# An attention and soft-mixture kernel: the value products' bank stored in two halves by two engines, and the inverse row sums kept in PSUM

## The chip, the cores and the metric

The kernel runs on one core of a Trainium2 chip. The metric is the device time of one execution in microseconds; lower is better. The engines are named as in the profile: PE is TensorE (matrix products and transposes, results in PSUM), DVE is VectorE, ACT is ScalarE, POOL is GpSimd, SP is SyncE, which here only issues DMAs. Each engine works through its own instructions in the order in which the program lists them. PSUM has banks of 512 float32 columns on 128 partitions.

## The reference

Eight batches of eight heads of windowed attention (576 positions, head size 64, window 128, a linear bias with the distance), then a soft mixture of experts over all 4608 tokens:

```python
scores = scale * np.matmul(q, k.transpose(0, 1, 3, 2))
scores = np.where(mask, scores + bias[None], -1000000000.0)   # mask: 0 <= i - j < 128
attn = np.exp(scores - np.max(scores, axis=-1, keepdims=True))
attn = attn / (np.sum(attn, axis=-1, keepdims=True) + 1e-09)
x = np.matmul(attn, v)                                        # -> tokens x 512
logits = x @ phi                                              # 32 slots, 4 for each expert
d = softmax over tokens;  slot_input = d.T @ x
slot_out[e] = np.maximum(slot_input[e] @ w1[e], 0.0) @ w2[e]
c = softmax over slots;   out = c @ slot_out
```

## The kernel before, in words

**Groups and turns.** A tile is 128 positions of one batch; each batch has four (t = 0 to 3) and a short tail tile of 64 (t = 4). The work goes by groups `(b, t, g)`: a full tile has two groups (g = 0 and 1) of four heads each, the tail tile has one with all eight. That makes nine groups a batch and 72 in all. The main loop makes one turn for each group `i`, and a turn works on several groups at once, at different stages. The order in which the loop's lines stand is the order on each engine; nothing is reordered.

**One turn**, after the first seven, lists:

1. `softmax_front` for the new group i and the old one i-1. On DVE: `merge` (L286, selects the valid score blocks, in PSUM), `rowmax` (L300, into a corner of the score bank), `inverse` of the old row sums (L313), `bias` (L304, the negated maximum times the scale), `normalise` of the old group (L317, the exponentials times the inverse sums, in SBUF). `total` (L309, row sum plus epsilon) runs on POOL.
2. `flip` of group i-3: PE transposes its probabilities into columns 0 to 255 of the two banks of `pq` (L374). Columns 256 to 511 of these banks take the transposed outputs of finished tiles (`x_flip`, L438).
3. `split` of group i-3: ACT copies the flipped probabilities to SBUF (L380), POOL masks them into two operands (L386, L388).
4. ACT work put down for this turn under "act": `x_keep` (L447, copies a flipped output tile to SBUF) and copies of the token steps (`token_copy` L464, `token_keep` L507).
5. `values` of group i-4: 16 products on PE (L410) into the bank `xp`. Then `after_values`.
6. `scores` of group i+1 on PE (L261 the bias terms, L270 the products) into one of two score buffers of two banks each, `s4_0` and `s4_1`, used in turn.
7. `expo` of group i: four ACT exponentials out of the score banks (L359), each with its row sum. It needs `bias` of this turn.
8. PE work put down under "pe": `x_flip` of a tile one turn or more after its last group's products, and, for every fourth tile, the token steps: `logits` (L456), `slot_flip` (L477) and `token_flip` (L502), both into a bank called `dp`, `slot_sum` (L514). On DVE, `slots_max` reads `dp` (L536, L537) and `slot_add` is L522.

**Values and their copy.** Both groups of a tile write the same bank `xp`, four pairs of heads side by side. When the second group (or the tail tile) is done, `x_store` copies the bank to SBUF on DVE (L424), in program order after the turn's normalisation. The next tile's first group takes a new `xp`, which is the same bank again.

**After the loop** the last groups are finished in an order written out by hand, in free score banks and in `pq`, and then come the experts' products with weights streamed in by DMA.

The row sums `rs` are a small SBUF tile; their inverse is written in place and read by `normalise` as an operand that is repeated over 128 columns.

## Time and profile before

| | before |
|---|---|
| time, median of 3 runs | 286.24 us (286.18 to 286.52) |
| the profiled execution's time | 286.09 us |
| its span, first to last instruction | 284.3 us |
| busy PE / DVE / ACT / POOL | 257.5 / 218.6 / 190.5 / 111.7 us |
| mean granted TensorE clock | 0.992 |
| bytes read / written in HBM | 62.30 / 9.44 MB |

The loop takes about the first 215 us of the span, the experts the rest. In rows of a timeline the columns are start, duration, engine, line, operation, output and inputs, count, and in brackets the idle time ahead of the instruction with what ended it. PEld is PE's loading of stationary operands, which runs beside its products. In rows of groups they are the shape and count, then busy time and mean ns of one, then the idle time ahead. In rows of waits: total us, times, longest. In rows of one window: start and end, length, busy time and count of PE, PEld, DVE, ACT and POOL (or of the one engine asked for), granted clock, share of DMA time, GB/s.

### The profile page before, as it was taken

To read this page: it belongs to the slowest core of one execution; us is meant where nothing else is said; L and a number is where in the kernel's file an instruction comes from. 1 tells how busy PE (TensorE), PEld (TensorE's weight loads), DVE (VectorE), ACT (ScalarE), POOL (GpSimd) and SP (SyncE) were. 2 spreads that over 40 slices of the span, in tenths; PEclk is the share of its full clock that TensorE was granted. 3 is DMA by queue.
4 is the path that set the end of the run, shared out by engine and by line. 5 is a ranking of instruction groups with operands and counts; after the bars stand their busy time and mean duration, and the time that the engine had idled before them with its cause. 6 is when DMAs were issued, how large, how long until landed. Compare 5 with 4: busy or idle time off the path is not lost.

```text
span 284.3 us, 11675 instructions
## 1 busy us (share of the span) xinstructions
PE 257.5 (91%) x4575; PEld 180.7 (64%) x4575; DVE 218.6 (77%) x546; ACT 190.5 (67%) x780; POOL 111.7 (39%) x221
## 2 busy tenths in 40 slices
PE   7789898989899999998989998998989899999990
PEld 3567676767577677676667766766666443587750
DVE  1789998997998898899999899897973352656352
ACT  2868868887798887897897888887774411044460
POOL 3035734481574385265527526556452011000000
PEclk9999999999999999999999999999999999999996
DMA  5735368889786998889698778876565588999997
GB/s 167 238 110 153 115 173 250 255 247 295 252 277 184 303 303 262 257 265 285 221 298 283 255 236 280 268 212 218 166 213 199 172 257 296 417 416 373 376 357 295
DMA packets 36767, 72.49 MB, mean 255 GB/s; under 512 B 4413, under 2 KB 15337, under 8 KB 36713
## 3 DMA queue, kind: packets, MB, share of 16 engines
q1 hardware_dynamic: 35992, 71.25, 75.7%
q8 instruction: 36, 0.59, 0.8%
q10 hardware_dynamic: 720, 0.51, 0.6%
q14 instruction: 19, 0.15, 0.2%
HBM read 62.30 MB, written 9.44 MB: 252 GB/s over the span
## 4 chain that ended last, share of the span: by engine, by line
PE 44%; DVE 38%; ACT 9%; issue 3%; DMA 3%; POOL 1%; DVEq 0%; ACTq 0%; SPq 0%; POOLq 0%
DVE area L317 12%; DVE s L300 9%; PE xp L410 8%; ACT area L359 6%; PE op L967 5%; PE s L270 5%; DVE area L424 5%; PE hp L930 5%; DVE s L286 4%; PE po L992 4%; PE s L261 2%; PE lp L456 2%; PE pq L374 2%; DVE acc L522 2%; DMA area<-v_n 2%
## 5 line engine op out<-in xcount | busy, mean ns | idle before, releaser
L359 ACT ACTIVATE area<-s,nb 128x128 f32<-128x128 f32 x286 | 101.9, 379 | 21.6 <-DVE nb L304 20.2
L410 PE MATMUL xp<-area 128*64 128x128 f32 (+1 forms) x1104 | 71.7, 270 | 9.5 <-DVE area L424 6.6
L410 PEld LDWEIGHTS xp<-area 128*64 128x64 f32 x1104 | 54.5, 137 | 16.4 <-POOL area L388 5.0
L359 ACT ACTIVATION_READ_ACCUMULATOR area<-s,nb 128x1 f32 x286 | 62.2, 218 | 0.0
L317 DVE TENSOR_TENSOR area<-area,rs 128x512 f32<-128x512 f32 (+1 forms) x73 | 59.9, 821 | 1.7 <-ACT area L447 0.4
L270 PE MATMUL s<-kq 64*64 64x192 f32 (+2 forms) x1144 | 57.0, 316 | 0.0
L386 POOL TENSOR_SCALAR_AFFINE_SELECT area<-area 128x512 f32<-128x512 f32 (+1 forms) x57 | 42.7, 748 | 26.9 <-ACT area L380 26.3
L380 ACT COPY area<-pq 128x512 f32<-128x512 f32 (+1 forms) x72 | 42.5, 592 | 16.0 <-PE pq L374 14.3
L300 DVE TENSOR_REDUCE s<-s 128x4 f32<-128x512 f32 (+1 forms) x72 | 50.0, 694 | 2.2
L388 POOL TENSOR_SCALAR_AFFINE_SELECT area<-area 128x512 f32<-128x512 f32 (+1 forms) x57 | 46.5, 817 | 3.9
L270 PEld LDWEIGHTS s<-kq 64*64 64x64 f32 x1144 | 41.2, 139 | 3.4
L309 POOL TENSOR_SCALAR rs<-sm 128x4 f32<-128x4 f32 x70 | 13.5, 193 | 71.2 <-ACT area L359 69.8
L286 DVE COPY_PREDICATED s<-cst,s 128x256 f32<-128x256 int32 (+1 forms) x72 | 30.2, 419 | 4.8 <-PE s L270 4.4
L374 PE MATMUL pq<-unit_r,area 64*128 64x64 f32 x552 | 31.4, 234 | 1.9 <-ACT area L322 1.2
L374 PEld LDWEIGHTS pq<-unit_r,area 64*128 64x128 f32 x552 | 23.0, 140 | 11.6 <-issue 5.0
L261 PE MATMUL s<-ramp,pair_of 64*64 64x384 bf16 x286 | 27.0, 358 | 2.5 <-ACT area L359 2.0
L424 DVE COPY area<-xp 128x512 f32<-128x512 f32 (+1 forms) x38 | 24.1, 633 | 3.6 <-PE xp L410 3.4
L447 ACT COPY area<-pq 128x512 f32<-128x512 f32 x34 | 20.2, 594 | 0.3 <-PE pq L432 0.3
L261 PEld LDWEIGHTS <-pair_of 64*64 64x64 bf16 x288 | 9.5, 106 | 15.7 <-issue 12.0
L438 PEld LDWEIGHTS pq<-unit_r,area 64*128 64x128 f32 x264 | 10.7, 138 | 13.2 <-issue 11.7
L994 ACT COPY ob<-po 128x512 f32<-128x512 f32 x19 | 10.4, 592 | 11.4 <-PE po L992 11.4
L994 DVE COPY ob<-po 128x512 f32<-128x512 f32 x17 | 11.2, 686 | 6.6 <-PE po L992 4.4
(164 smaller groups left out, 276.6 us busy)
## 6 DMA issues: line engine op xcount, KB each, us to landing
w<-w SPq DMA_DIRECT2D x53, 512.0 KB, 5.4
out<-ob SPq DMA_DIRECT2D x36, 256.0 KB, 3.6
kq<-q_t SPq DMA_DIRECT2D x69, 128.0 KB, 3.3
kq<-k_t SPq DMA_DIRECT2D x32, 256.0 KB, 3.4
area<-v_n SPq DMA_DIRECT2D x31, 256.0 KB, 4.5
area<-w SPq DMA_DIRECT2D x8, 512.0 KB, 4.9
area<-v_n SPq DMA_DIRECT2D x12, 128.0 KB, 5.2
kq<-w SPq DMA_DIRECT2D x3, 512.0 KB, 5.6
```

The lines of the kernel that those rows point to most:

```text
L261: nc.tensor.matmul(dst[strip], lhsT=pair_of[rows, int(t == 0), strip], rhs=src, start=True, stop=False)
L270: nc.tensor.matmul(parts[par][KB * jj:KB * jj + KB, second * u + KB * skip:second * u + WIN], lhsT=qt[rows, jj if t < 4 else j, KB * h:KB ...
L286: nc.vector.copy_predicated(to, keep, of)
L300: nc.vector.tensor_reduce(st[key]["mx"], merged(key, us), axis=AX.X, op=ALU.max, negate=True)
L317: nc.vector.tensor_tensor(p4, p4, bc(rs, 2, P), op=ALU.mult)
L359: nc.scalar.activation(s["p4"][:, u], src, AF.Exp, bias=s["nb"][:, u:u + 1], scale=SCALE, accum_out=s["sm"][:, u:u + 1],)
L374: nc.tensor.transpose(s["pt"][:, 2 * (u % 2) + u // 2, r], s["p4"][rows, u], ident[rows, rows])
L380: nc.scalar.copy(pa[:, us].rearrange("p u (r w) -> p u r w", r=2), s["pt"][:, us])
L386: nc.gpsimd.affine_select(prev, own, [[-step, m], [0, 4], [-1, KB]], ALU.is_gt, 0.0, base=-i0, channel_multiplier=1)
L388: nc.gpsimd.affine_select(own, own, [[step, m], [0, 4], [1, KB]], ALU.is_ge, 0.0, base=i0, channel_multiplier=-1)
L410: nc.tensor.matmul(xp[D * par:D * par + D, j, 0:w], lhsT=v_slot[b, t - 1 + ph][:, D * h:D * h + D], rhs=src[:, :, par, i] if t < 4 else sr ...
L424: nc.vector.tensor_copy(dst, src[:, :, 0:w])
```

## The change

1. One tile `xp` is kept for the whole loop as two halves of 256 columns. Group number n writes half n mod 2, with a fresh start of its own sum, and each group's half is copied by itself. The copy of a first group (g = 0 of a full tile) is put down for the next turn under "act" and runs on ScalarE, after whatever was put down there before. The copy of a second group or of a tail tile stays on VectorE, in its own turn, with half the columns.
2. From the third turn on the inverse row sums of the old group are written to columns 504 to 507 of the new group's first score bank, and `normalise` reads them there.
3. After the loop each copy names its group; that of tile 3's second group has half the columns.

```diff
-    def inverse(key, us):
-        nc.vector.reciprocal(st[key]["rs"][:, us], st[key]["rs"][:, us])
+    def inverse(key, us, beside=None):
+        sums = st[key]["rs"]
+        if beside is not None:
+            st[key]["rs"] = st[beside]["s4"][:, 0, 4 * P - 8:4 * P - 4]
+        nc.vector.reciprocal(st[key]["rs"][:, us], sums[:, us])
...
-            inverse(old, ALL)
+            inverse(old, ALL, new)
...
     def values(key, pairs=None, to=None):
-        if (b, t) not in st or to is not None:
-            st[b, t] = ps_1.tile([P, NPAIR, P], F32, tag="xp", name="xp") if to is None else to
-        xp = st[b, t]
+        if ("x", key) in st:
+            xp = st["x", key]
+        elif to is None:
+            if not xp_bank:
+                xp_bank.append(ps_1.tile([P, 2, 2 * P], F32, tag="xp", name="xp"))
+            xp = xp_bank[0][:, number[key] % 2].rearrange("p (j w) -> p j w", j=2 if t < 4 else 4)
+        else:
+            xp = to[:, 2 * g:2 * g + 2] if t < 4 else to
+        st["x", key] = xp
...
-                        xp[D * par:D * par + D, j, 0:w], lhsT=v_slot[b, t - 1 + ph][:, D * h:D * h + D],
+                        xp[D * par:D * par + D, i, 0:w], lhsT=v_slot[b, t - 1 + ph][:, D * h:D * h + D],
...
-                        start=(fresh and (ph, i) == (parts[0], inner[0])), stop=(done and (ph, i) == (parts[-1], inner[-1])),
+                        start=((ph, i) == (parts[0], inner[0])), stop=((ph, i) == (parts[-1], inner[-1])),
...
-    def x_store(b, t, eng=None, js=slice(0, NPAIR)):
-        src = st[b, t][:, js]
+    def x_store(key, eng=None):
+        b, t, g = key
+        src = st.pop(("x", key))
...
-        dst = x_of(b, t)[:, js, o:o + w]
+        dst = x_of(b, t)[:, 2 * g:2 * g + src.shape[1], o:o + w]
...
     def after_values(i, key):
         b, t, g = key
+        if g == 0 and t < 4 and i + 1 < n:
+            do("act", i + 1, x_store, key, nc.scalar)
+        else:
+            x_store(key)
         if not (g == 1 or t == 4):
             return
...
-        x_store(b, t)
...
-        x_store(last, 3)
+        x_store(ga)
...
-        x_store(last, 4, nc.scalar)
+        x_store(gb, nc.scalar)
...
-        x_store(last, 0, nc.scalar, slice(0, 2))
+        x_store(gc, nc.scalar)
...
-        x_store(last, 0, js=slice(2, 4))
+        x_store(gd)
```

## The prediction

> **What bounds the kernel now.** The page first, for the span and the shares; then one window over the attention loop, whole and for the row maximum alone, which runs once for each group of heads and so counts the turns.

> ```profile
> span 284.3 us, 11675 instructions
> PE 257.5 (91%) x4575; PEld 180.7 (64%) x4575; DVE 218.6 (77%) x546; ACT 190.5 (67%) x780; POOL 111.7 (39%) x221
> PE 44%; DVE 38%; ACT 9%; issue 3%; DMA 3%; POOL 1%; DVEq 0%; ACTq 0%; SPq 0%; POOLq 0%
> L410 PE MATMUL xp<-area 128*64 128x128 f32 (+1 forms) x1104 | 71.7, 270 | 9.5 <-DVE area L424 6.6
> 30.00:210.00 180.00, 169.53 (x3331) 123.79 (x3331) 164.44 (x404) 146.85 (x639) 95.64 (x180) 1.00 0.77 243
> 30.00:210.00 180.00, 43.96 (x63) 1.00 0.77 243
> ```

> From 30 to 210 us TensorE is busy for 169.53 of 180 us (the first busy column), so PE is idle for 10.5 us in the whole stretch. 63 turns in 180 us make 2.86 us a turn, 5.7 us for the two turns of one tile. The chain divides itself between PE and DVE, but there is little slack in PE: what the change can give back in the loop is at most those idle microseconds, and a new wait of PE is paid nearly in full. Of the idle time, 9.5 us over the whole run lie ahead of the value products (L410), 6.6 of it because the bank's copy on VectorE (L424) is not done. That wait is what the halves speak to.

> **Does the program let two engines work in one bank at different columns?** All of the change hangs on this. Three places in the timeline show it, where the columns differ and no data is shared.

> ```profile
> 92.55 0.33 PE L502 MATMUL dp<-unit_r,lg 128*128 128x128 f32 x1
> 92.91 0.29 DVE L536 TENSOR_REDUCE cm<-dp 128x4 f32<-128x128 f32 x1 [0.39 <-PE dp L502]
> ...
> 138.06 0.66 ACT L380 COPY area<-pq 128x512 f32<-128x512 f32 x1
> 138.30 0.29 DVE L537 TENSOR_TENSOR ln<-dp,cm 128x128 f32<-128x128 f32 x1
> 138.62 0.27 ACT L507 COPY dn<-dp 128x128 f32<-128x128 f32 x1
> ...
> 97.22 0.58 ACT L447 COPY area<-pq 128x512 f32<-128x512 f32 x1
> 97.88 0.33 PEld L374 LDWEIGHTS pq<-unit_r,area 64*128 64x128 f32 x8 [0.28 <-ACT area L447]
> ...
> PEld pq L374 <- ACT area L447: 2.3, 9, 0.3
> ```

> L536 reads columns 256 up of dp, which another product wrote a turn before; L502 writes columns 0 to 127. L536 starts 0.03 us after L502 ends (92.88). So a read waits for a write elsewhere in its bank. L507 reads columns 0 to 127 of the same bank while L537 reads 256 up: it starts 0.03 us after L537 ends (138.59), so two reads wait for each other too. L374 writes pq's columns 0 to 255 while L447 reads 256 to 511, and waits for it 9 times. That is the situation of the two halves of xp, one engine on each. [...]

> **The change part by part.**

> *The first group's copy, on ScalarE.* It is put behind the split (L380) and the keep (L447) of the next turn, and ahead of that turn's value products in the program. Those write the other half of the bank, so they now wait for ScalarE. Before, the second group added into the same bank and waited for no copy. The stretch of a second group:

> ```profile
> 112.51 0.46 PE L374 MATMUL pq<-unit_r,area 64*128 64x64 f32 x8
> 112.89 1.10 PE L410 MATMUL xp<-area 128*64 128x128 f32 x16
> 113.08 0.59 ACT L380 COPY area<-pq 128x512 f32<-128x512 f32 x1 [1.22 <-PE pq L374]
> 113.57 0.59 ACT L447 COPY area<-pq 128x512 f32<-128x512 f32 x1
> ...
> L380 ACT COPY area<-pq 128x256 f32<-128x256 f32 x3 | 1.0, 368 | 0.7 <-PE pq L369 0.7
> ...
> 108.32 0.68 DVE L424 COPY area<-xp 128x512 f32<-128x512 f32 x1
> 109.14 1.09 PE L410 MATMUL xp<-area 128*64 128x128 f32 x16 [0.70 <-DVE area L424]
> ```

> PE's flip ends at 112.97, ScalarE had been waiting for it for 1.22 us, the split starts at 113.08, the keep at 113.57 (0.49 later), a copy of half the bank would start at 114.06 and take 0.37 (the 128x256 row), and PE starts some 0.1 us after a copy (0.14 at 109.14). So the products would start at 114.5 instead of 112.89: 1.6 us of PE standing still, with the scores, the next flip and everything else of PE queued behind it in order. ScalarE cannot do the copy earlier, though it idled: the copy is queued behind the split, and the split needs the flip. This happens for the first groups of tiles 0 to 3 in seven batches and of two tiles of the last: 30 times, 30 x 1.6 = 48 us. Bounds: where ScalarE has no keep in that turn the wait is 1.1 us (33 us in all); where ScalarE comes late from its exponentials, as in the stretch shown further down (split at 101.68, products at 101.14), it is 2.0 us (60 us). I take 1.6, the case where ScalarE waits for PE, since PE is the busy one. Where copies of the token steps (L464, L507, some 0.25 us each) also precede the store, I add 2 us in all; the bounds are 0 and 4 (15 of them).

> *The second group's copy, on VectorE, of half the size.* It still ends ahead of the next tile's products. It is shorter, and VectorE gains time in a turn that has become longer: I cost it at nothing, hidden by PE's new wait. If that cover is gone it is a gain within the 6.6 us.

> *Waits that go.* In a pair that is 1.6 us longer, VectorE's copy and GpSimd's selects are done in time. Of the 9.5 us ahead of L410 I take 8 off; bounds 0 and the 10.5 us of all idle time.

> *Row sums in PSUM.* The reciprocal writes into a corner of the new group's first score bank, and the normalisation reads it there. ScalarE's exponentials read that bank. So by L507's row the first exponential waits for the end of the normalisation, not for the bias (L304) as now. The stretch:

> ```profile
> 98.85 0.42 DVE L286 COPY_PREDICATED s<-cst,s 128x256 f32<-128x256 int32 x1
> 100.04 0.16 DVE L304 TENSOR_SCALAR nb<-s 128x4 f32<-128x4 f32 x1
> 100.19 0.76 DVE L317 TENSOR_TENSOR area<-area,rs 128x512 f32<-128x512 f32 x1
> 100.30 0.37 ACT L359 ACTIVATE area<-s,nb 128x128 f32<-128x128 f32 x1 [0.62 <-DVE nb L304]
> 101.14 1.09 PE L410 MATMUL xp<-area 128*64 128x128 f32 x16
> 101.68 0.59 ACT L380 COPY area<-pq 128x512 f32<-128x512 f32 x1
> 102.11 0.18 DVE L313 RECIPROCAL rs<-rs 128x4 f32<-128x4 f32 x1
> 102.17 0.36 PE L261 MATMUL s<-ramp,pair_of 64*64 64x384 bf16 x4
> 102.36 0.82 PE L270 MATMUL s<-kq 64*64 64x192 f32 x16
> 102.40 0.79 DVE L317 TENSOR_TENSOR area<-area,rs 128x512 f32<-128x512 f32 x1
> ...
> L317 DVE TENSOR_TENSOR area<-area,rs x73: 415/695/1192, 10.3 to 213.7; 128x512 f32<-128x512 f32 x70, 128x256 f32<-128x256 f32 x3
> L522 DVE SCALAR_TENSOR_TENSOR acc<-acc,al,ap x7: 732/739/740, 78.2 to 207.9; 128x512 f32<-128x512 f32 x6, 96x512 f32<-96x512 f32 x1
> ```

> For the new form I take L522, two streams of 128x512, one of them from PSUM: 0.74 us every time, where L317 runs from 0.69 to 1.19. The first exponential then starts about 0.75 us later than now. What does that cost? Two rings. (a) Normalisation ends, 0.1 to the exponential, 1.81 to the reciprocal of the same group (100.30 to 102.11), 0.29 on to the next normalisation (102.11 to 102.40), 0.74: 2.94 us a turn at least, against 2.86 on average now. (b) The ring through both parts of the change: products to scores 1.03, scores 1.01 (102.17 to 103.18), 0.1, merge to normalisation 1.34 (98.85 to 100.19), 0.74, 0.1, four exponentials 1.38 (100.30 to 101.68), split 0.49, keep 0.49, copy 0.37, 0.1: 7.15 us for two turns. By PE's new wait alone the pair takes 5.7 + 1.6 = 7.3, so (a), with 5.9, is covered, and (b) decides only in pairs without token work on PE, which are shorter than the mean. I estimate 12 such pairs at 0.4: +5 us; bounds 0 and +12 (1.0 each, if PE's own pair were 6.2).

> *The tail.* Each of its copies is of half a bank as before, but ga's, which halves: -0.3, nothing.

> Sum against the profiled execution's own 286.1 (span 284.3; the median of the runs is 286.24, 0.1 above): 286.1 + 48 + 2 + 5 - 8 = 333.

> **The rivals.**

> *Row sums alone (304 us).* The halves cost nothing because the waits fall where PE stood anyway, and ring (a) rules, in 69 turns. Against the mean of 2.86 its 2.94 costs +6. But turns differ, as the row maxima of five show:

> ```profile
> 99.31 0.70 DVE L300 TENSOR_REDUCE s<-s 128x4 f32<-128x512 f32 x1
> 101.40 0.68 DVE L300 TENSOR_REDUCE s<-s 128x4 f32<-128x512 f32 x1
> 104.16 0.70 DVE L300 TENSOR_REDUCE s<-s 128x4 f32<-128x512 f32 x1
> 106.35 0.70 DVE L300 TENSOR_REDUCE s<-s 128x4 f32<-128x512 f32 x1
> 109.37 0.70 DVE L300 TENSOR_REDUCE s<-s 128x4 f32<-128x512 f32 x1
> ...
> L317 DVE TENSOR_TENSOR area<-area,rs 128x512 f32<-128x512 f32 (+1 forms) x73 | 59.9, 821 | 1.7 <-ACT area L447 0.4
> ```

> Turns of 2.09, 2.76, 2.19 and 3.02 us, the first three lifted to 2.94 and the last kept, are 1.8 longer, 0.44 a turn, +30 in all. Middle: +18, 304. For it: VectorE's normalisation has 12% of the chain. Against it: PE's wait for a copy behind the flip can't fall where it stood, since PE itself makes the flip just before.

> *Side by side (279 us).* The other side: accesses to different columns of one bank do not wait in this code, PE writes one half while the other is stored. Then the 6.6 us ahead of L410 go: 286.1 - 6.6 = 279.5, and at most 10.5 go. It decides if value products start before the other half's copy has ended. Against it stand the three pairs of rows above.

> *The port (280 us).* The normalisation gets shorter and that carries. Beside a GpSimd select L317 runs up to 1.19, L522 holds 0.74 throughout; the mean of L317 is 821 ns (the row above), so 73 x 0.082 = 6 us of VectorE go: 280, if all of it lay on the path and no exponential waited. The median, 0.695, speaks against it, as more than half of the instructions get longer. [...]

> *Nothing moves (286 us).* ScalarE's copy falls into its idle time (146.85 busy of 180 in the window), and what VectorE saves pays for the rest. It would need the copy to end before PE has finished its flip, and the queue order forbids that.

> **How the numbers follow.** Forecast 0.79 (its own range 316 to 348: by the bounds of the wait, 33 to 60, and of the ring); row sums alone 0.08; side by side 0.07; the port 0.03; nothing moves 0.03. The predicted time is the forecast's, 333. The range goes from 297, which takes in the row-sums case with its own low side, to 350, just over the forecast's own; out of it fall the last three cases (0.13) and some hundredths of the others. Faster 0.10, same 0.03, slower 0.87, with 0.2% as about the least that a measurement of this kernel can tell from no change.

> **What would show it.** In the profile after: PE's value products (L410 of before) wait for ScalarE's new copy some 30 times, 40 us or more in all; ScalarE has 30 copies of 128x256 at 0.37; the wait of the exponentials names the normalisation rather than the bias, in most of the turns; the normalisation's spread closes to near 0.74 and GpSimd's selects become shorter; PE's idle time between 30 us and the loop's end grows from 10 to some 50 us; the rest after the loop keeps its length. Wrong I am if products into one half start while the other half's copy runs, or if ScalarE's copy comes ahead of the split.

## The result and the profile after

The changed kernel takes 353.8 us (median; 348.8 to 355.5), the kernel before 286.2 us in the same runs. The ratio, formed from undisturbed runs alone, is 1.2297, with a 95% interval from 1.2237 to 1.2356, or 352 us. The direction was as forecast; 333 us was too little, and the range ended at 350. The profiled execution took 348.8 us at a mean granted clock of 0.943. It is the shortest of the six; others from which the ratio is formed took 351.6 us at 0.933, 353.6 at 0.924 and 354.0 at 0.919, so the time grows as the clock falls.

First the page of the changed kernel: span and shares, the clock row of its forty slices, the chain, three groups of instructions. Line numbers have moved: L416 are the value products, L433 and L431 the copies of the halves on ScalarE and VectorE, L362 the exponentials, L320 the normalisation, L383 and L456 the split and the keep, L377 the flip.

```profile
span 347.1 us, 11745 instructions
PE 271.4 (78%) x4575; PEld 190.8 (55%) x4575; DVE 209.4 (60%) x547; ACT 202.3 (58%) x810; POOL 97.2 (28%) x221
PEclk9999698889989999898999988999999999999996
PE 51%; ACT 23%; DVE 15%; issue 5%; DMA 2%; POOL 1%; DVEq 0%; ACTq 0%; SPq 0%; POOLq 0%
L362 ACT ACTIVATE area<-s,nb 128x128 f32<-128x128 f32 x286 | 101.7, 371 | 44.7 <-DVE area L320 40.6
L416 PE MATMUL xp<-area 128*64 128x128 f32 (+1 forms) x1104 | 77.5, 286 | 58.0 <-ACT area L433 55.2
L320 DVE TENSOR_TENSOR area<-area,s 128x512 f32<-128x512 f32 x69 | 46.8, 678 | 0.0
```

The clock row of the kernel before:

```profile
PEclk9999999999999999999999999999999999999996
```

PE runs the same 4575 products as before. Its idle time went from 284.3 - 257.5 = 26.8 us to 347.1 - 271.4 = 75.7 us, +48.9. Its busy time went from 257.5 to 271.4 us, +13.9. Together that is the whole growth of the span, 62.8 us, and it lies in the loop: from the start of the last exponential to the end it is 73.2 us before and 73.3 after. The idle time stands ahead of the value products (58.0 us, 9.5 before), and the clock row is no longer an unbroken line of nines.

The waits of the changed kernel (total us, times, longest):

```profile
PE xp L416 <- ACT area L433: 55.2, 29, 2.6
ACT area L362 <- DVE area L320: 40.6, 40, 3.0
```

One pair of groups in its timeline, from a flip to the products of the next first group:

```profile
136.28 0.41 PE L377 MATMUL pq<-unit_r,area 64*128 64x64 f32 x8
136.43 0.37 ACT L362 ACTIVATE area<-s,nb 128x128 f32<-128x128 f32 x1 [1.31 <-DVE area L320]
137.82 0.59 ACT L383 COPY area<-pq 128x512 f32<-128x512 f32 x1
138.29 0.62 ACT L456 COPY area<-pq 128x512 f32<-128x512 f32 x1
138.76 0.41 ACT L433 COPY area<-xp 128x256 f32<-128x256 f32 x1
139.32 1.09 PE L416 MATMUL xp<-area 128*64 128x128 f32 x16 [2.62 <-ACT area L433]
140.34 0.53 PE L261 MATMUL s<-ramp,pair_of 64*64 64x384 bf16 x4
142.07 1.90 PE L416 MATMUL xp<-area 128*64 128x128 f32 x16
```

PE has flipped by 136.69 and stands until 139.32, behind four exponentials, split, keep and copy. That is ring (b) of the prediction from the normalisation on, which the first exponential waited for. Then comes what the prediction did not have. The next sixteen products, the same work, take 1.90 instead of 1.09 us. Two windows of 5 us (length; busy time and count of PE, PEld, DVE, ACT, POOL; granted clock; DMA) show why:

```profile
135.00:140.00 5.00, 2.38 (x57) 1.91 (x55) 3.18 (x9) 3.26 (x15) 2.84 (x5) 1.00 0.79 239
140.00:145.00 5.00, 5.00 (x76) 3.70 (x74) 2.51 (x7) 2.76 (x15) 1.52 (x3) 0.66 0.51 161
```

PE was busy for 2.38 of 5 us, and in the next 5 us the granted clock is 0.66 on the mean; the last section lays the two stretches on the steps of the clock. From 30 to 210 us the mean is 0.91, where it was 1.00 before:

```profile
30.00:210.00 180.00, 136.53 (x2466) 100.15 (x2462) 115.43 (x298) 119.61 (x505) 60.99 (x132) 0.91 0.60 187
```

### The profile page after: what moved, and what is told of

Read it like the earlier page. It is cut to its first block, busy times and chain, and to the rows that moved or that the text cites. A ratio compares the mean times of both kernels' runs of the same rounds, so it can differ in the third digit from the quotient of the medians.

```text
span 347.1 us, 11745 instructions
## 1 busy us (share of the span) xinstructions
PE 271.4 (78%) x4575; PEld 190.8 (55%) x4575; DVE 209.4 (60%) x547; ACT 202.3 (58%) x810; POOL 97.2 (28%) x221
## 4 chain that ended last, share of the span: by engine, by line
PE 51%; ACT 23%; DVE 15%; issue 5%; DMA 2%; POOL 1%; DVEq 0%; ACTq 0%; SPq 0%; POOLq 0%
PE xp L416 14%; ACT area L362 11%; PE s L270 9%; ACT area L383 5%; PE op L979 4%; PE hp L942 4%; PE s L261 4%; DVE s L300 4%; DVE area L320 3%; ACT area L456 3%; PE pq L377 3%; PE po L1004 3%; ACT area L433 2%; DVE s L286 2%; PE lp L465 1%
## 5 line engine op out<-in xcount | busy, mean ns | idle before, releaser
L362 ACT ACTIVATE area<-s,nb 128x128 f32<-128x128 f32 x286 | 101.7, 371 | 44.7 <-DVE area L320 40.6
L416 PE MATMUL xp<-area 128*64 128x128 f32 (+1 forms) x1104 | 77.5, 286 | 58.0 <-ACT area L433 55.2
L416 PEld LDWEIGHTS xp<-area 128*64 128x64 f32 x1104 | 60.7, 147 | 64.7 <-POOL area L389 31.0
L383 ACT COPY area<-pq 128x512 f32<-128x512 f32 (+1 forms) x72 | 41.7, 581 | 43.9 <-PE pq L377 40.4
L270 PE MATMUL s<-kq 64*64 64x192 f32 (+2 forms) x1144 | 60.8, 333 | 0.0
L362 ACT ACTIVATION_READ_ACCUMULATOR area<-s,nb 128x1 f32 x286 | 59.6, 208 | 0.0
L389 POOL TENSOR_SCALAR_AFFINE_SELECT area<-area 128x512 f32<-128x512 f32 (+1 forms) x57 | 37.3, 654 | 52.3 <-ACT area L383 52.0
L300 DVE TENSOR_REDUCE s<-s 128x4 f32<-128x512 f32 (+1 forms) x72 | 50.0, 694 | 2.2
L320 DVE TENSOR_TENSOR area<-area,s 128x512 f32<-128x512 f32 x69 | 46.8, 678 | 0.0
L270 PEld LDWEIGHTS s<-kq 64*64 64x64 f32 x1144 | 43.4, 148 | 4.7
L286 DVE COPY_PREDICATED s<-cst,s 128x256 f32<-128x256 int32 (+1 forms) x72 | 30.5, 424 | 21.6 <-PE s L270 21.1
L431 DVE COPY area<-xp 128x256 f32<-128x256 f32 x39 | 16.5, 423 | 37.8 <-PE xp L416 36.0
L391 POOL TENSOR_SCALAR_AFFINE_SELECT area<-area 128x512 f32<-128x512 f32 (+1 forms) x57 | 37.3, 655 | 3.9
L377 PE MATMUL pq<-unit_r,area 64*128 64x64 f32 x552 | 33.3, 244 | 1.5 <-ACT area L325 1.3
L377 PEld LDWEIGHTS pq<-unit_r,area 64*128 64x128 f32 x552 | 24.6, 149 | 12.2 <-issue 7.5
L261 PE MATMUL s<-ramp,pair_of 64*64 64x384 bf16 x286 | 28.5, 380 | 2.7 <-ACT area L362 2.3
L316 DVE RECIPROCAL s<-rs 128x4 f32<-128x4 f32 x69 | 12.8, 186 | 19.9 <-POOL rs L309 15.4
L456 ACT COPY area<-pq 128x512 f32<-128x512 f32 x34 | 20.3, 598 | 0.3 <-PE pq L441 0.3
L261 PEld LDWEIGHTS <-pair_of 64*64 64x64 bf16 x288 | 9.5, 108 | 16.6 <-issue 15.1
L447 PEld LDWEIGHTS pq<-unit_r,area 64*128 64x128 f32 x264 | 11.1, 142 | 13.3 <-issue 12.7
L1006 ACT COPY ob<-po 128x512 f32<-128x512 f32 x19 | 10.3, 591 | 11.5 <-PE po L1004 9.7
```

The lines of the kernel that those rows point to most:

```text
L261: nc.tensor.matmul(dst[strip], lhsT=pair_of[rows, int(t == 0), strip], rhs=src, start=True, stop=False)
L270: nc.tensor.matmul(parts[par][KB * jj:KB * jj + KB, second * u + KB * skip:second * u + WIN], lhsT=qt[rows, jj if t < 4 else j, KB * h:KB ...
L286: nc.vector.copy_predicated(to, keep, of)
L300: nc.vector.tensor_reduce(st[key]["mx"], merged(key, us), axis=AX.X, op=ALU.max, negate=True)
L320: nc.vector.tensor_tensor(p4, p4, bc(rs, 2, P), op=ALU.mult)
L362: nc.scalar.activation(s["p4"][:, u], src, AF.Exp, bias=s["nb"][:, u:u + 1], scale=SCALE, accum_out=s["sm"][:, u:u + 1],)
```

## The experiments

The theory: PE's wait for ScalarE's copy makes the 49 us of idle time; the waiting exponentials lengthen it; the 14 us of busy time are PE's clock, cut after it has stood. Rivals: the row sums carry the loss; the products are longer for another reason; any copy between the two groups is as dear.

**The halves alone**

```diff
-            inverse(old, ALL, new)
+            inverse(old, ALL)
```

> The two halves as in the change, the inverse row sums back in SBUF. Theory (PE's wait for ScalarE's copy carries the loss, the exponentials' wait for the normalisation only lengthens it): the ring through both is about 0.75 us a pair shorter, so PE waits about 1.6 instead of 2 us at each of 30 places; PE's idle time grows by 35 to 40 us instead of 49, the exponentials wait for the bias again, and with the shorter waits the granted clock is at or above 0.95. Time 325 to 338. Rival (the row sums carry it): 286 to 300.

Measured: 332.1 us, ratio 1.158 [1.153, 1.163].

```profile
PE 265.6 (80%) x4575; PEld 186.7 (56%) x4575; DVE 216.1 (65%) x547; ACT 201.1 (61%) x810; POOL 112.5 (34%) x221
PE xp L416 <- ACT area L433: 49.5, 30, 2.0
```

Thirty waits of 1.65 us: the prediction's 30 x 1.6. The halves are some 46 us of the loss by themselves. PE's idle time is 331.0 - 265.6 = 65.4 us, 38.6 over that of before; its busy time is already 8 us over, at a mean clock of 0.951.

**The row sums alone** (in the kernel before; `[:, 0]` is the first bank)

```diff
-            inverse(old, ALL)
+            inverse(old, ALL, new)      # writes s4 of new, [:, 0, 504:508]
```

> The kernel before with only the inverse row sums moved into the first score bank. Theory: the exponentials wait for the normalisation in nearly all turns, a turn has a floor of 2.9 us, and PE's waits are short and spread, so the clock stays at 0.99: 292 to 308, the number I gave this as a rival being 304. Rival (row sums carry the change's loss): above 320. Second rival (shorter normalisation and faster selects pay for it): 282 to 287.

Measured: 299.9 us, ratio 1.048 [1.044, 1.052]: the prediction's rival for this part was 304. The waits, and the normalisation and first select by their full shape:

```profile
ACT area L362 <- DVE area L320: 41.1, 55, 1.4
DVE s L316 <- POOL rs L309: 22.8, 43, 0.8
L320 DVE TENSOR_TENSOR area<-area,s 128x512 f32<-128x512 f32 x69 | 46.7, 677 | 0.0
L389 POOL TENSOR_SCALAR_AFFINE_SELECT area<-area 128x512 f32<-128x512 f32 x55 | 36.4, 662 | 15.5 <-ACT area L383 15.0 <-PE xp L413 0.5
```

The exponentials wait for the normalisation, and the reciprocal then waits for the sums: ring (a). The normalisation is indeed shorter, 0.677 us against 0.838 on the mean before, and the select with it, 0.662 against 0.761:

```profile
L317 DVE TENSOR_TENSOR area<-area,rs 128x512 f32<-128x512 f32 x70 | 58.7, 838 | 1.4 <-ACT area L447 0.4
L386 POOL TENSOR_SCALAR_AFFINE_SELECT area<-area 128x512 f32<-128x512 f32 x55 | 41.8, 761 | 24.8 <-ACT area L380 24.2
```

No gain in time came of it; the exponentials now begin only at the normalisation's end. I had expected the clock to stay at 0.99; it was 0.980, with PE busy for 261.5 us, 4 more than before. By themselves the two parts cost 46 and 14 us, together 66: on top of the halves, the row sums cost 20.

**Unused products in PE's wait** (in the changed kernel)

```diff
+    def fill(i):                        # ahead of values() in the turn of a second group
+        ...
+        for par in (0, 1, 0, 1):
+            to = s4s[(i + 1) % 2][:, 2 * par:2 * par + 2].rearrange("p u w -> p (u w)")
+            nc.tensor.matmul(to, lhsT=pair_of[:, 0], rhs=ramp.rearrange("p g w -> p (g w)"), start=True, stop=True)
```

> The changed kernel with four more bf16 products (128x512, into the score bank that the next scores overwrite, result unused) ahead of the value products of each second group, where PE stands waiting for ScalarE's copy. Theory (PE's busy time grew by 14 us because its clock is cut while it stands): the clock is back at 0.98 or more, the products' durations are those of the kernel before, and the time falls by 8 to 14 us, to 335 to 342, although PE has some 120 more products. Rival (the products are longer for another reason, such as engines meeting in PSUM): the clock figure may rise, the time does not fall: 348 to 356.

Measured: 342.2 us, ratio 1.1975 [1.192, 1.203], against the change's 1.2297 [1.224, 1.236]. The intervals are apart by 2% of the time before at the least, the middles by 9 us. The time is at the upper end of what I expected, the mean clock, 0.973, a little under it. L427 is the added line (90 of its 120 products have a record).

```profile
PE 286.8 (84%) x4665; PEld 192.2 (56%) x4695; DVE 209.1 (61%) x547; ACT 202.0 (59%) x810; POOL 97.1 (29%) x221
L427 PE MATMUL s<-ramp,pair_of 128*128 128x512 bf16 x90 | 29.8, 386 | 23.1 <-ACT area L362 21.0
L416 PE MATMUL xp<-area 128*64 128x128 f32 x880 | 64.0, 285 | 11.7 <-ACT area L441 9.2 <-POOL area L389 1.2 <-DMA area<-v_n 1.2
```

The PE time without the added line is 286.8 - 29.8 = 257.0 us, that of the kernel before (257.5). More work on PE made the kernel faster. The product's long form is at 285 ns, 302 in the change and 282 before. The unused products are not free: PE's idle time and they come to 53.6 + 29.8 = 83.4 us, 7.7 more than the idle time of the change.

**The same in the halves alone**

> The halves alone (row sums in SBUF), with the four unused bf16 products ahead of each second group's value products. Theory of the clock: PE's busy time without the unused products falls from 265.6 to 257 or 258, that of the kernel before, and the time from 332 by 4 to 8, to 324 to 328. Rival: PE's products stay as long as they were and the time is 331 or more.

Measured: 325.0 us, ratio 1.136 [1.134, 1.139], against 1.158 [1.153, 1.163] without. The page and the window:

```profile
PE 286.5 (89%) x4695; PEld 191.1 (59%) x4695; DVE 215.9 (67%) x547; ACT 201.0 (62%) x810; POOL 113.2 (35%) x221
L427 PE MATMUL s<-ramp,pair_of 128*128 128x512 bf16 x120 | 30.8, 379 | 5.9 <-ACT area L362 5.1
30.00:210.00 180.00, 163.80 (x2903) 111.32 (x2900) 136.99 (x339) 132.30 (x562) 79.76 (x148) 1.00 0.67 210
```

286.5 - 30.8 = 255.7 us, at a clock of 1.00 in the loop, where the halves without the unused products had 265.6 us. The mean clock over the span went from 0.951 to 0.996. So the added busy time is the clock, and here the clock rose when PE was kept busier.

**ScalarE's copy ahead of the split** (in the changed kernel)

```diff
-            do("act", i + 1, x_store, key, nc.scalar)
+            do("ahead", i + 1, x_store, key, nc.scalar)
...
+            run("ahead", i)             # first thing after softmax_front
             near = int(i < SKIP)
```

> The changed kernel with ScalarE's copy put ahead of the split and the keep of the same turn, nothing else. Theory (the place in ScalarE's queue makes the wait long, the same-bank wait itself is cheap): PE waits for the copy without 0.98 us of split and keep and without its own flip: waits under 0.8 us, clock above 0.97, time 300 to 315. Rival (any wait of one half for the other costs about as much): above 335.

Measured: 310.7 us, ratio 1.082 [1.076, 1.089]. Same copy, same engine, same bank: the place in the queue is worth some 42 us. PE's idle time ahead of the products is 30.1 us (58.0 in the change), about 1 us a pair, 1.8 at the longest, where I had expected under 0.8, and the clock, 0.966, is a little under the 0.97 expected. The timeline shows one of the short waits:

```profile
L416 PE MATMUL xp<-area 128*64 128x128 f32 x880 | 65.2, 289 | 30.1 <-POOL rs L309 20.6 <-ACT area L433 8.3 <-DMA area<-v_n 1.0
124.76 0.38 ACT L433 COPY area<-xp 128x256 f32<-128x256 f32 x1
124.97 0.19 POOL L309 TENSOR_SCALAR rs<-sm 128x4 f32<-128x4 f32 x1 [1.25 <-ACT area L362]
125.29 1.09 PE L416 MATMUL xp<-area 128*64 128x128 f32 x16 [0.19 <-POOL rs L309]
```

The row names GpSimd's row sum, but the products do not use it; the copy ended at 125.14 and the sum at 125.16, and such a wait is put down to the later of the two. The copy is now right behind the exponentials, and these wait for the normalisation, 38.5 us in all. The copy ahead of the split with the row sums in SBUF was not run.

**Both copies on VectorE, in the turn of their products** (row sums in SBUF)

```diff
-        if g == 0 and t < 4 and i + 1 < n:
-            do("act", i + 1, x_store, key, nc.scalar)
-        else:
-            x_store(key)
+        x_store(key)
```

> The two halves, each copied by VectorE in the turn of its products, row sums in SBUF as before. VectorE has one copy of 0.42 us in every turn in place of one of 0.68 in every second, and the second group's products wait for a copy at the end of the turn before. Theory (a wait of one half for the other costs by what stands ahead of the copy; on VectorE that is a normalisation that ends early in PE's turn): 288 to 298, the clock at 0.98 or more. Rival (a copy between the two groups is as dear on any engine): above 310.

Measured: 285.7 us, ratio 0.9996 [0.998, 1.002], under the range that I expected.

```profile
span 284.3 us, 11714 instructions
PE 258.5 (91%) x4575; PEld 180.7 (64%) x4575; DVE 220.9 (78%) x577; ACT 190.9 (67%) x780; POOL 112.4 (40%) x221
```

The value products wait for the copy for 2.9 us in all (6.6 before), and the time is that of before. So neither the halves nor the wait between two groups need cost anything, as long as the copy ends before PE comes to the products. Engine and turn were changed together here; ScalarE's copy in the turn of its own products was not run. 31 more instructions on VectorE are hidden too.

**Row sums in the second score bank** (in the kernel before; the edit is shown against the run with the first bank)

```diff
-            st[key]["rs"] = st[beside]["s4"][:, 0, 4 * P - 8:4 * P - 4]
+            st[key]["rs"] = st[beside]["s4"][:, 1, 4 * P - 8:4 * P - 4]
```

> The kernel before with only the inverse row sums moved into the new group's second score bank instead of the first. The first two exponentials read the first bank and need not wait; the third starts about 0.7 us after the first, when the normalisation (0.68 us) has just ended. Theory (the 14 us of the row sums alone are the exponentials' wait for the bank): nearly all of it goes, and the evenly short normalisation and selects remain: 281 to 287. Rival (the operand in PSUM costs by itself, or any exponential's wait costs as much): 295 to 301.

Measured: 299.1 us, ratio 1.046 [1.043, 1.050], as in the first bank: a miss. Its timeline has the bias, the normalisation and the first exponential, which reads the first bank:

```profile
105.55 0.16 DVE L304 TENSOR_SCALAR nb<-s 128x4 f32<-128x4 f32 x1
105.63 0.68 DVE L320 TENSOR_TENSOR area<-area,s 128x512 f32<-128x512 f32 x1
106.40 0.37 ACT L362 ACTIVATE area<-s,nb 128x128 f32<-128x128 f32 x1 [1.42 <-DVE area L320]
```

The exponential still starts after the normalisation (106.31), not after the bias (105.71), though they are in different banks. The two banks are one tile of the program, and its waits here follow the tile. Whether the chip would need the wait was not tried.

**The two repairs together: copy ahead of the split, row sums in the second bank**

> The changed kernel with ScalarE's copy ahead of the split and the inverse row sums in the second score bank. Theory: the two repairs are of different waits and add up: 310.7 less 8 to 14, 296 to 303, still over the kernel before because the second group's products wait for a copy that was not there. Rival (once the copy is out of the way the rest costs nothing): 283 to 289.

Measured: ratio 1.088 [1.083, 1.093], or 311 us; with the sums in the first bank it was 1.082 [1.076, 1.089]. No gain, a miss, and what the run before it would make one expect. No version tried beats the kernel before.

## Why the prediction was wrong in size and right in kind

*Engines in one bank take turns, whatever the columns.* Right for the waits of this program: PE waited 29 times, 55.2 us in all, for the copy of the other half, and the exponentials 40 times, 40.6 us, for the normalisation. What two engines would do in one bank without such waits, no run shows. And one of the three rows did not show it: the copy at 138.62 (L507) has no idle time ahead of it and stands right behind the split in ScalarE's queue. The same copy at another place of that trace does show it:

```profile
47.54 0.29 DVE L537 TENSOR_TENSOR ln<-dp,cm 128x128 f32<-128x128 f32 x1
47.86 0.27 ACT L507 COPY dn<-dp 128x128 f32<-128x128 f32 x1 [0.22 <-DVE ln L537]
```

And all the rows were inside one tile: I said "bank" where in the second-bank run the exponential out of the first bank still started only at 106.40, after the normalisation's end at 106.31, so that there the wait covers the tile. The two halves as two tiles were not run.

*PE's wait for ScalarE's copy: 48, with 2 and 5 us from token copies and ring (b).* Right: 55 was the sum, 55.2 us were measured in 29 waits of 1.9; without the row sums 49.5 in 30 of 1.65, where 48 + 2 = 50 was forecast. The copy took 0.40 instead of 0.37.

*Waits that go: 8.* Nearly right: 9.5 us of idle time ahead of the products before, 58.0 - 55.2 = 2.8 us of others after, so 6.7 went.

*Row sums: covered by the pair's length, but for ring (b): 5.* Half right. The exponentials wait as said, and the sums took PE's waits from 1.65 to 1.9 us, 5.7 us in all, with the longest at 2.6 instead of 2.0. The normalisation is 0.68 us, not the 0.74 taken from L522. But on top of the halves the sums cost not 5 but 20 us by the ratios. In the profiled executions it is 16: PE's idle time went from 65.4 to 75.7 us, 10.3, and its busy time from 265.6 to 271.4, with the clock from 0.951 to 0.943.

*What failed is a step that had no term: "286.1 + ...", PE's own work at its old length.* The sum forecast 47 us of idle time and got 48.9. That this is so close is in part luck: the halves' share came out at 38.6 where 42 was forecast, the row sums' at 10.3 where 5 was. PE's 257.5 us of work were carried over unchanged, and became 271.4. The missing 13.9 us and the 1.9 us beside them are 333 to 348.8, the profiled execution's time; the other executions ran at lower clocks still. I wrote "PE standing still" thirty times over and read a clock of 1.00 from a kernel whose PE had been 94% busy in that stretch. The trace before had one place to warn of it, the 6 at the end of its clock row: PE's last product ends at 277.35, and from 279.78 the granted clock is 0.50 (windows of the kernel before):

```profile
276.36:279.78 3.42, 0.99 (x3) 0.37 (x2) 2.39 (x4) 0.44 (x1) 0.00 (x0) 1.00 1.05 403
279.78:283.19 3.41, 0.00 (x0) 0.00 (x0) 0.00 (x0) 0.00 (x0) 0.00 (x0) 0.50 0.81 310
```

The bounds of the single terms did not become the range either: they add up to 309 and 362, where the forecast's own range was 316 to 348. With the clock held by unused products the halves alone take 325 us, where 286.1 + 48 + 2 - 8 = 328 is this part's share of the sum. For the whole change they leave 342 against 333.

*The rivals.* "Row sums alone" gave 304 for that part by itself and the part measured 300. "Side by side" fell with the 29 waits. "The port", the rival of the shorter normalisation, had its effect right, 0.838 to 0.678 us and the select from 0.761 to 0.662, though no run shows why they became shorter, and its conclusion wrong. "Nothing moves" gave the time of the copies on VectorE, but by another way than ScalarE's idle time.

## What to carry to other kernels

A copy that frees a buffer belongs in a queue where nothing stands ahead of it that its consumer produces: here the place in ScalarE's queue was worth 42 us, and the halves by themselves cost nothing. Before an operand goes into a corner of a live PSUM tile, list who else reads that tile: in the row sums alone the exponentials waited 55 times, 41.1 us in all, for the normalisation, which like them only reads the score bank. And when a change makes PE wait regularly, cost its remaining work as well, not only the waits: look for stretches in which it is busy for less than about half, as in the last section.

## What the runs showed of the hardware that I had not expected

In the changed kernel PE's clock was cut to 0.50 in nine stretches of 3.41 or 6.83 us between 34 and 213 us, though no wait of PE for the copy was longer than 2.6 us. PE's rows from 35 us:

```profile
35.45 1.98 PE L416 MATMUL xp<-area 128*64 128x128 f32 x16 [2.30 <-ACT area L433]
39.08 1.97 PE L416 MATMUL xp<-area 128*64 128x128 f32 x16
44.41 1.09 PE L416 MATMUL xp<-area 128*64 128x128 f32 x16 [1.61 <-ACT area L433]
...
35.00:40.00 5.00, 4.55 (x54) 3.72 (x56) 2.49 (x7) 2.40 (x11) 1.59 (x4) 0.50 0.17 45
```

In the window the clock is 0.50, and the same sixteen products take 1.98 us, at full clock 1.09. The 0.66 over 5 us above is a step at 0.50, from 140.36 to 143.77, and the rest at full clock: (3.41 x 0.50 + 1.59) / 5.

The traces show roughly at what busy share the cuts came. In those of the kernel before and of the changed kernel the changes of the granted clock lie whole multiples of 3.41 us apart (3.41, 6.83, 13.65, 17.07 us and more). Windows laid on these steps give PE's busy time in the step before a cut, 1.15 and 1.04 us here, and then the cut itself:

```profile
31.13:34.54 3.41, 1.15 (x28) 0.77 (x27) 1.98 (x5) 2.99 (x15) 1.52 (x3) 1.00 0.42 127
34.54:37.96 3.42, 2.52 (x32) 2.13 (x36) 1.37 (x4) 2.27 (x11) 1.71 (x4) 0.50 0.03 8
136.94:140.36 3.42, 1.04 (x20) 0.90 (x20) 1.41 (x4) 2.99 (x14) 1.52 (x3) 1.00 0.68 213
140.36:143.77 3.41, 3.41 (x46) 2.75 (x44) 2.42 (x6) 1.34 (x6) 0.98 (x3) 0.50 0.43 118
```
